# Moving the second half of a nested closing unit behind the next slot's first unit, its GpSimd adds behind the copy of x, and four weight differences one slot earlier

## The chip, the cores and the metric

The kernel runs on one core of one Trainium2 chip. The metric is the device time of one execution in microseconds (us); the median of 3 runs of the kernel before is 207.39 us (207.31 to 207.75). Times with a place, such as "94.92", are microseconds from the start of the profiled span of the kernel before.

## The reference, cut to what matters

Two blocks follow each other. The first is a cross attention without projections between `x` (8 batches, 8 heads, 512 rows, 64 wide) and `state` (32 rows per head), in both directions. The second is one exact-GELU feed-forward layer on all 4352 rows, 512 to 2048 to 512 wide.

```
a  = softmax(x @ state.T / sqrt(64));   xread = a @ state      # 512 rows per batch
a2 = softmax(state @ x.T / sqrt(64));   sread = a2 @ x         # 32 rows per batch
rows = concat([xread, sread]) with the heads side by side      # (8*544) x 512
out  = gelu_exact(rows @ w_in) @ w_out                         # (8*544) x 512
```

## The kernel before, in words

**Slots and pairs.** The work is written out by hand, engine by engine, in the order of the calls; no scheduler moves it. The main loop (L1240) has one slot for each batch b = 2 to 7, and a slot has eight pairs p = 0 to 7. In a pair `M(k, k+1)` runs two of the sixteen chunks of the first layer: `mm1` (L501) does two 128x512 matmuls of the folded weights `P` with the transposed attention `AT` into one PSUM tile `hp`, and ScalarE's GELU (L513) writes a chunk of `g`. Four PSUM buffers, tag "f", are handed out in turn to `hp`, to the scores `pt`, to the small transposes `srT` and to others: the fifth request waits until the first buffer has been read.

**The second layer, one slot later.** While slot b makes its own `g`, its pairs also multiply the `g` of batch b - 1 by `w_out`. This is done with seven products of half-size quarters in place of eight (Strassen in Winograd's form). A product is called a unit, "1" to "7"; `X(b, name)` (L676) runs one as 16 matmuls of 128x256 (`x_mm`, L648) into one of four PSUM banks (`BANK`, L667). Units "1", "6" and "7" add up in bank 1, "5" and "3" in bank 2, "2" has bank 0, "4" bank 3. What goes into "5", "6", "7" and "3" are sums of quarters of `g`, made on VectorE by `g_sum` (L633, tile `gsum`, three buffers); VectorE also adds PSUM and saved parts into the output tile `oh` (L670). Pairs 0 to 3 of a slot run units "1", "6", "5", "7" of the batch before, pair 5 unit "3".

**Nested units.** Units "2" and "4" of the later batches are themselves done with seven quarter-size products of 4 matmuls each, 128x128 (`sub_mm`, L728). Unit "4" belongs to batch 3 and later. It has three parts. `sub_sums` (L720) makes the sums of `g` (tile `gsub`). `sub_a` (L742) runs four products into the four parts of the bank, and ScalarE copies the bank to `qa` (L747). `sub_b` (L749) runs the other three products onto the same bank, ScalarE copies it to `qb` (L755), and three adds (L765) join `qa` and `qb` into `c2` or `c4`: on VectorE for unit "2", on GpSimd for unit "4". `qa`, `qb`, `c2` and `c4` have one buffer each, shared by both units. The sub-products need differences of weights, `q_w`, made once by four VectorE subtractions for each unit (`w_subs`, L590).

**Order around the change.** In slot b: pair 3 has `sub_sums(b, "2")`; pair 5 `sub_a(b, "2")` and `sub_sums(b, "4")`; pair 6 `sub_b(b, "2")`; pair 7 `sub_a(b, "4")`. Pair 0 of slot b + 1 has `M`, then `sub_b(b, "4")`, then `g_sum` of "5" and "6", then unit "1". Pair 1 starts with the scores of the next batch (`scores`, L325: exponentials on ScalarE, L340, with a load of its activation table before them and another before the next GELU), pair 2 and 3 have `norm` (L347: reduce, reciprocal, product `a<-e,ics` at L356), pair 2 of an odd slot the transposes `srT` (`srts`, L421). `c4` is read by `c21` (L709) after unit "7" in pair 3. Slot 7 has its own order for pairs 0 to 4 (`read_out_slot`, L1044), where the 32 read-out rows of all batches go through the same layer: `SR` (L862) with sums `srx` (L842), `srw` (L825) and `srt` (L885 to L898).

**GpSimd's queue.** GpSimd also brings in `x`: `hold_for` (L1032) waits for a given GELU, `load_x` (L115) issues the 512 KB load `xb`, `rearr` (L221, copies at L225) and `rearr_ones` (L230, copies at L235) copy it into the two layouts `x` and `xo`. In pair 0 of a slot the order on GpSimd is: the adds of unit "4", `hold_for` and `load_x`, `rearr` of batch b + 2.

Of the kernel before, what the change touches and what calls it, by code (L numbers as in the profile page):

```python
# [9 lines left out]
FP32 = mybir.dt.float32  # L10
# [7 lines left out]
def kernel(  # L18
# [562 lines left out]
    QN = NH // 2  # L581
# [94 lines left out]
    def X(b, name):  # L676
        bank = BANK[name]
        first = name in "2154"
        if first:
            xs[b, bank] = otile([128, 2, NH], "xp", bank)  # L680
        ps = xs[b, bank]
        x_mm(ps, x_lhs(b, name), w_rhs(name), first)
        if name == "2":
            if b > 1:
                snap(b, "c2", "c2", ps)
        elif name == "4":
            snap(b, "c4", "c4", ps)
        elif name == "1":
            for h in range(2):
                xs[b, "o", h] = hpool.tile([128, 2, d_model], FP32, name="oh", tag=f"oh{h}")  # L690
            add(xs[b, "o", 0][:, :, left], ps, xs[b, "c2"])
            x_out(b, 0, left)
        elif name == "6":
            snap(b, "u", "u", ps)
        elif name == "5":
            snap(b, "s5", "c2", ps)
        elif name == "7":
            if b < B - 2:
                c22(b)
                c21(b)  # L700
                x_out(b, 1)
        elif name == "3":
            add(xs[b, "o", 0][:, :, right], ps, xs[b, "u"])
            x_out(b, 0, right)
# [44 lines left out]
    def sub_b(b, unit):  # L749
        sub_mm(b, unit, "6", 1)  # L750
        sub_mm(b, unit, "3", 3)
        sub_mm(b, unit, "7", 0, True)
        qa = xs[b, "qa"]
        qb = cpool.tile([128, 4, QN], FP32, name="qb", tag="qb")
        nc.scalar.copy(out=qb, in_=xs[b, BANK[unit]])  # L755
        name = "c" + unit
        c = xs[b, name] = c_tile(name)
        c = c.rearrange("p j (n w) -> p j n w", n=2)
        wide = [128, 2, QN]
        for out, x, y in (  # L760
            (c[:, 0], qb[:, 1:2, :].broadcast_to(wide), qb[:, 0:4:3, :]),
            (c[:, 1], c[:, 0, 0:1, :].broadcast_to(wide), qa[:, 2:4, :]),
            (c[:, 0, 0, :], qa[:, 1, :], qa[:, 0, :]),
        ):
            (nc.vector if unit == "2" else nc.gpsimd).tensor_tensor(out=out, in0=x, in1=y, op=ALU.add)  # L765
# [76 lines left out]
    def sr_x(names):  # L842
        for name in names:
            if "x" not in sr:
                t = att.tile([128, 4, 2, TH], BF16, name="srx", tag="e")
                one = att.tile([128, 2, TH], BF16, name="srx1", tag="a")
                sr["x"] = dict(zip("34167", [t[:, i] for i in range(4)] + [one]))
            (k0, n0), (k1, n1), op = {
                "3": ((0, 1), (1, 1), ALU.subtract),
                "4": ((1, 0), (0, 0), ALU.subtract),  # L850
                "6": ((0, 0), (0, 1), ALU.add),
                "1": ((0, 0), (1, 1), ALU.add),
                "7": ((1, 0), (1, 1), ALU.add),
            }[name]
            nc.vector.tensor_tensor(
                out=sr["x"][name], in0=sr_xq(k0, n0), in1=sr_xq(k1, n1), op=op
            )
# [186 lines left out]
    def read_out_slot(p):  # L1044
        c, b, k = B - 2, B - 1, 16 * (B - 1) + 2 * p
        if p == 0:
            sr_x("34")
            M(k, k + 1)
            sub_b(c, "4")
            g_sum(c, "56")  # L1050
            SR("3", 0)
            SR("4", 0)
            X(c, "1")
            sr_x("167")
            SR("5", 0)
            SR("2", 0)
            sr_w("7")
        if p == 1:
            M(k, k + 1)
            SR_gelu("52", 0)  # L1060
            X(c, "6")
            SR("1", 0)
            SR("6", 0)
        if p == 2:
            M(k, k + 1)
            SR_gelu("6", 0)
            SR("7", 0)
            SR_gelu("7", 0)
            g_sum(c, "7")
            X(c, "5")  # L1070
            SR("3", 1)
            SR("4", 1)
            g_sum(c, "3")
        if p == 3:
            M(k, k + 1)
            SR("5", 1)
            SR("2", 1)
            SR_gelu("52", 1)
            X(c, "7")
            c22(c)  # L1080
            SR("1", 1)
            c21(c)
            x_out(c, 1)
            SR("6", 1)
        if p == 4:
            M(k, k + 1)
            SR_gelu("6", 1)
            SR("7", 1)
            SR_gelu("7", 1)
            X(c, "3")  # L1090
# [149 lines left out]
    for b in range(2, B):  # L1240
        nb = b + 1
        for p in range(8):
            k = 16 * b + 2 * p
            if p == 1 and nb < B:
                scores(nb, 0)
                scores(nb, 1)
            if p in (2, 3) and nb < B and (b > 2 or p == 2):
                norm(nb, p - 2)
            if p == 3 and nb + 1 < B:
                xtr_dma(nb + 1)  # L1250
            if p == 5 and nb < B:
                atr_dma(nb)
            if nb == B and p < 5:
                read_out_slot(p)
                if p == 4:
                    r_homes()
                    r_sum("56")
                continue
            late = p == 5 and b % 2 and nb < B
            if late:  # L1260
                M(k)
            elif b != 2 or p != 3:
                M(k, k + 1)
            if b == 2 and p == 2:
                M(k + 2, k + 3)
            if b == 2 and p == 1:
                w_diff("7")
            if p < 5 and nb < B:
                if p == 0:
                    if b > 3:  # L1270
                        sub_b(b - 1, "4")
                    g_sum(b - 1, "56")
                if p == 2:
                    if b % 2:
                        srts((b - 1, b))
                    g_sum(b - 1, "7")
                if p == 3:
                    g_sum(b - 1, "3")
                if p < 4:
                    X(b - 1, "1657"[p])  # L1280
                if p == 3:
                    sub_sums(b, "2")
                    if b == 3:
                        w_subs("4", range(4))
                if b == 2 and p == 2:
                    norm(3, 1)
                    for x in [(2, f, p_mm(2, f, ftile)) for f in (2, 3)]:
                        p_copy(*x)
                if p == 1 and b > 2:
                    sr_w("5216"[b - 3])  # L1290
            if p == 0 and b + 3 < B:
                hold_for(b, 0)
                load_x(4 if b == 2 else b + 3)
            if p == 6 and b == 2:
                hold_for(b, 12)
                load_x(5)
            if p == 0 and nb + 1 < B:
                begin(nb + 1)
                rearr(nb + 1)
            if nb == B:  # L1300
                if p == 5:
                    R("2")
                    r_sum("73")
                    R("4")
                    sub_sums(b, "2")
                if p == 6:
                    R("1")
                    sub_a(b, "2")
                    R("6")
                    sub_b(b, "2")  # L1310
                    R("5")
                if p == 7:
                    X(b, "4")
                continue
            if p == 5:
                X(b - 1, "3")
                if late:
                    M(k + 1)
                reads = (b, nb) if b % 2 == 0 else ()
                rest = p_all(nb, reads)  # L1320
                if b == 2:
                    rearr_ones(4)
                elif nb + 1 < B:
                    if not reads:
                        hold_for(b, 11)
                    rearr_ones(nb + 1)
                sub_a(b, "2")
                if b > 2:
                    sub_sums(b, "4")
                for _, f, ps in rest:  # L1330
                    nc.scalar.copy(out=Ps[nb][:, 0, f * 512:(f + 1) * 512], in_=ps[0])
            if p == 6:
                sub_b(b, "2")
            if p == 7:
                if nb == B - 1:
                    srts(reads)
                if b > 2:
                    sub_a(b, "4")
                else:
                    X(b, "4")  # L1340
# [43 lines left out]
```

## Time and profile before

| | us |
|---|---|
| median of 3 runs (lowest, highest) | 207.39 (207.31, 207.75) |
| the profiled execution's own time | 207.22 |
| its span, first to last instruction | 205.4 |
| TensorE (PE) busy | 194.1 (94% of the span) |
| VectorE (DVE) busy | 163.3 (80%) |
| ScalarE (ACT) busy | 147.8 (72%) |
| GpSimd (POOL) busy | 58.2 (28%) |
| granted TensorE clock, mean | 1.000 |

The lines of the timeline read: start, length, engine, line of the code, operation, output<-inputs, shapes, count of merged instructions, and in square brackets how long the engine had been idle before and on what. A matmul's length holds the time through the array, so the next one starts before its end; what a group of matmuls costs TensorE is the distance from its start to the start of the next group. By that measure in slot 4: a pair `M` 0.86, a whole unit 1.75, the scores 0.47, a `sub_b` 0.67 (94.92 to 95.59). "PEld" is the load of weights, "SPq" the queue that issues transfers.

### The profile page before, as it was taken

The numbers are of one execution on the slowest core, as the hardware profiler recorded it, in microseconds if no ns is written. First come the engines' busy times: TensorE is split into PE (matmuls) and PEld (weight loads), VectorE is DVE, ScalarE is ACT, GpSimd is POOL, SyncE is SP. The second block draws the span as 40 slices with busy tenths as digits, with TensorE's granted clock in tenths as the row PEclk, the third lists the DMA queues.
The fourth block names the chain that finished last, engine by engine and source line by source line (L and its number), as shares of the span: only waits on it lengthen the run. The fifth ranks groups of instructions, "written<-read, shape, count | busy, mean of one in ns | idle before, by whom it ended". The sixth has DMA issues, their size and how long they took to land.

```text
span 205.4 us, 5204 instructions
## 1 busy us (share of the span) xinstructions
PE 194.1 (94%) x2155; PEld 134.0 (65%) x2155; DVE 163.3 (80%) x299; ACT 147.8 (72%) x268; POOL 58.2 (28%) x77
## 2 busy tenths in 40 slices
PE   7899999999999999988999899989999899999992
PEld 2434544466766777656767577657776688878891
DVE  2954895889988699986998889978977987984952
ACT  3775678798984998489966996689849778765120
POOL 8972503634332423041803081213000220000000
PEclk9999999999999999999999999999999999999999
DMA  6999999988467899440597015821033010030153
GB/s 199 197 168 203 209 196 188 186 145 149 52 121 192 120 119 215 133 99 3 95 160 207 2 56 102 130 77 39 15 121 86 3 51 3 35 120 3 51 154 108
DMA packets 40569, 23.19 MB, mean 113 GB/s; under 512 B 21856, under 2 KB 39136, under 8 KB 40544
## 3 DMA queue, kind: packets, MB, share of 16 engines
q0 software_dynamic: 13984, 8.10, 29.4%
q1 hardware_dynamic: 25728, 14.22, 28.1%
q10 hardware_dynamic: 832, 0.52, 0.8%
q8 instruction: 17, 0.28, 0.6%
q14 instruction: 8, 0.07, 0.1%
HBM read 17.30 MB, written 8.91 MB: 128 GB/s over the span
## 4 chain that ended last, share of the span: by engine, by line
PE 78%; ACT 5%; DMA 5%; DVE 5%; POOL 4%; issue 1%; ACTq 0%; POOLq 0%; DVEq 0%
PE xp L651 31%; PE hp L506 22%; PE xp L733 7%; DMA xb<-in_x_dram 5%; PE op L548 4%; PE sp L877 3%; PE rp L949 3%; DVE c L765 2%; POOL w_in_bf L105 2%; PE op L532 2%; PE xp L784 2%; PE pt L333 2%; ACT g L513 2%; PE p_ps L441 1%; ACT qa L747 1%; PE sr L979 1%
## 5 line engine op out<-in xcount | busy, mean ns | idle before, releaser
L513 ACT ACTIVATE g<-hp 128x512 bf16<-128x512 f32 x124 | 67.1, 613 | 16.9 <-PE hp L506 16.7
L506 PE MATMUL hp<-AT,P 128*128 128x512 bf16 x248 | 62.2, 379 | 0.0
L651 PEld LDWEIGHTS <-gsum 128*128 128x128 bf16 x416 | 40.4, 98 | 8.9 <-issue 0.4
L651 PE MATMUL xp<-ws,gsum 128*128 128x256 bf16 x320 | 38.2, 273 | 0.0
L506 PEld LDWEIGHTS <-P 128*128 128x128 bf16 x248 | 22.8, 98 | 19.3 <-ACT P L452 0.7
L670 DVE TENSOR_TENSOR oh<-xp,c 128x512 f32<-128x512 f32 (+1 forms) x22 | 14.2, 663 | 6.7 <-PE xp L651 5.1
L651 PEld LDWEIGHTS <-g 128*128 128x128 bf16 x176 | 16.9, 98 | 2.7
L225 POOL COPY x<-xb 128x1024 bf16<-128x1024 bf16 x12 | 12.6, 1080 | 18.5 <-DMA xb<-in_x_dram 18.5
L641 DVE TENSOR_TENSOR gsum<-g 128x2048 bf16<-128x2048 bf16 x14 | 17.0, 1217 | 0.6 <-ACT g L513 0.6
L235 POOL COPY xo<-xb 128x1024 bf16<-128x1024 bf16 x12 | 12.2, 1047 | 11.8 <-PE sr L979 11.6
L651 PE MATMUL xp<-w_out_bf,g 128*128 128x256 bf16 x128 | 15.3, 273 | 0.0
L733 PE MATMUL xp<-q_w,gsub 128*128 128x128 bf16 x120 | 11.6, 219 | 3.6 <-ACT qa L747 3.6
L765 POOL TENSOR_TENSOR c<-qb 128x256 f32<-128x256 f32 x4 | 3.7, 923 | 39.8 <-ACT qb L755 39.8
L733 PEld LDWEIGHTS <-gsub 128*128 128x128 bf16 x160 | 10.2, 97 | 6.6 <-issue 5.3
L356 DVE TENSOR_TENSOR a<-e,ics 128x512 bf16<-128x512 bf16 x14 | 12.6, 900 | 0.5
L548 PE MATMUL op<-w_out_bf,g 128*128 128x512 bf16 x48 | 11.8, 380 | 0.0
L651 PE MATMUL xp<-w_out_bf,gsum 128*128 128x256 bf16 x96 | 11.5, 272 | 0.0
L1019 DVE CAST P<-p_ps 128x512 bf16<-128x512 f32 x15 | 9.4, 684 | 2.1 <-PE p_ps L441 2.1
L1033 POOL COPY hold<-g 128x1 bf16<-128x1 bf16 x7 | 2.8, 404 | 28.7 <-ACT g L513 28.7
L353 DVE TENSOR_REDUCE cs<-e 128x16 f32<-128x512 bf16 x14 | 9.5, 677 | 0.7 <-ACT e L340 0.7
L441 PE MATMUL p_ps<-w_in_bf,sbd 64*32 64x512 bf16 x248 | 9.2, 380 | 0.7 <-DVE oh L670 0.7
L674 ACT COPY c<-xp 128x512 f32<-128x512 f32 x10 | 6.0, 596 | 4.8 <-PE xp L651 4.6
(156 smaller groups left out, 334.3 us busy)
## 6 DMA issues: line engine op xcount, KB each, us to landing
out_dram<-oh SPq DMA_DIRECT2D x15, 256.0 KB, 2.7
xb<-in_x_dram POOLq DMA_DIRECT2D x7, 512.0 KB, 6.9
out_dram<-oh SPq DMA_DIRECT2D x6, 512.0 KB, 3.3
w_in_bf<-in_moe_w_in_dram POOLq DMA_DIRECT2D x6, 256.0 KB, 12.2
out_dram<-osb SPq DMA_DIRECT2D x5, 256.0 KB, 2.9
w_out_bf<-in_moe_w_out_dram POOLq DMA_DIRECT2D x4, 256.0 KB, 7.8
w_out_bf<-in_moe_w_out_dram POOLq DMA_DIRECT2D x2, 512.0 KB, 13.6
x0f<-in_x_dram SPq DMA_DIRECT2D x3, 256.0 KB, 3.9
```

Of the source, the lines that this page charges most:

```text
L225: nc.gpsimd.tensor_copy(out=A.x4[:, :, :, 64 * t:64 * t + 64].rearrange("p j c d -> p c j d"), in_=src[:, t],)
L235: eng.tensor_copy(out=A.xo[:, :, :, 2 + 64 * t:66 + 64 * t].rearrange("p j c d -> p c j d"), in_=src[:, t],)
L353: nc.vector.reduce_sum(out=cs, in_=e4, axis=AX.X)
L356: nc.vector.tensor_tensor(out=A.a[:, :, hs].rearrange("p g (c n) -> p g c n", n=NS), in0=e4, in1=ics[:, :, :].to_broadcast((128, G, 2, NS) ...
L441: nc.tensor.matmul(ps[t][32 * c:32 * c + 32, :], lhsT=sbd[64 * t:64 * t + 64, b, c, 32 * t:32 * t + 32], rhs=w_in_bf[64 * t:64 * t + 64, c ...
L506: nc.tensor.matmul(hp, lhsT=Ps[b][:, t, m * 128:(m + 1) * 128], rhs=atts[b].AT[:, :, t, :], start=(t == 0), stop=(t == 1),)
L513: nc.scalar.activation(out=gs[b][:, m, :], in_=hp, func=AF.Gelu)
L548: nc.tensor.matmul(ops[b, j], lhsT=gs[b][:, m, j * 128:(j + 1) * 128], rhs=w_out_bf[:, m, :], start=(m == 0), stop=(m == MC - 1),)
L641: nc.vector.tensor_tensor(out=got[name], in0=x, in1=y, op=op)
L651: nc.tensor.matmul(ps[:, j - js[0], :], lhsT=lhs[:, m, 128 * j:128 * j + 128], rhs=rhs[:, m, :], start=(first and j == js[0] and m == 0), ...
L670: nc.vector.tensor_tensor(out=out, in0=x, in1=y, op=ALU.add)
L733: nc.tensor.matmul(xs[b, BANK[unit]][:, at, :], lhsT=lhs[:, m, :], rhs=rhs[:, m, :], start=(start and m == 0), stop=(m == MH // 2 - 1), sk ...
```

## The change

`sub_b` is cut in two: the matmuls and ScalarE's copy to `qb` stay in it, the three adds become `sub_c`. For unit "2" both are called where `sub_b` was. For unit "4":

- in slots 4 to 6, `sub_b(b - 1, "4")` moves from before `g_sum` and unit "1" to after unit "1" of pair 0; `sub_c(b - 1, "4")` goes to pair 1, after unit "6", and so stands behind `hold_for`, `load_x` and `rearr` in GpSimd's queue (slot 5 has only `rearr`, slot 6 none of the three);
- in slot 7 (`read_out_slot`) both move behind `SR("3")`, `SR("4")` and unit "1";
- `w_subs("4", range(4))`, the four weight differences, moves from pair 3 of slot 3 to pair 6 of slot 2, ahead of `sub_b(2, "2")`.

No instruction is added or taken away on any engine, and no transfer.

```diff
         sub_mm(b, unit, "7", 0, True)
-        qa = xs[b, "qa"]
-        qb = cpool.tile([128, 4, QN], FP32, name="qb", tag="qb")
+        qb = xs[b, "qb"] = cpool.tile([128, 4, QN], FP32, name="qb", tag="qb")
         nc.scalar.copy(out=qb, in_=xs[b, BANK[unit]])
+
+    def sub_c(b, unit):
+        qa, qb = xs[b, "qa"], xs[b, "qb"]
         name = "c" + unit
...
             M(k, k + 1)
-            sub_b(c, "4")
             g_sum(c, "56")
             SR("3", 0)
             SR("4", 0)
             X(c, "1")
+            sub_b(c, "4")
+            sub_c(c, "4")
             sr_x("167")
...
                 if p == 0:
-                    if b > 3:
-                        sub_b(b - 1, "4")
                     g_sum(b - 1, "56")
...
                     X(b - 1, "1657"[p])
+                if b > 3 and p == 0:
+                    sub_b(b - 1, "4")
+                if b > 3 and p == 1:
+                    sub_c(b - 1, "4")
                 if p == 3:
                     sub_sums(b, "2")
-                    if b == 3:
-                        w_subs("4", range(4))
...
                     sub_b(b, "2")
+                    sub_c(b, "2")
...
             if p == 6:
+                if b == 2:
+                    w_subs("4", range(4))
                 sub_b(b, "2")
+                sub_c(b, "2")
```

## The prediction

> **What bounds the kernel now.** First the page's busy times: TensorE works 194.1 of 205.4 us, so what counts is where it waits. Then the list of waits, TensorE's part:
>
> ```profile
> PE xp L733 <- ACT qa L747: 3.6, 4, 0.9
> ...
> PE p_ps L441 <- DVE oh L670: 0.7, 1, 0.7
> ```
>
> Behind the start-up these five are all. Then the timeline around them. Slots 3 and 4:
>
> ```profile
> 86.19 0.42 DVE L599 TENSOR_TENSOR q_w<-ws 128x512 bf16<-128x512 bf16 x1
> ...
> 87.66 0.68 DVE L670 TENSOR_TENSOR oh<-xp,u 128x512 f32<-128x512 f32 x1
> ...
> 88.40 0.41 PE L441 MATMUL p_ps<-w_in_bf,sbd 64*32 64x512 bf16 x8 [0.72 <-DVE oh L670]
> ...
> 92.96 1.03 PE L506 MATMUL hp<-AT,P 128*128 128x512 bf16 x4
> ...
> 94.29 0.59 ACT L747 COPY qa<-xp 128x512 f32<-128x512 f32 x1 [0.36 <-DVE c L765]
> ...
> 94.92 0.38 PE L733 MATMUL xp<-q_w,gsub 128*128 128x128 bf16 x4 [0.94 <-ACT qa L747]
> ```
>
> At 88.40 a matmul waits for a VectorE add that stands behind the four weight differences. At 94.92 `sub_b` waits for the `qa` copy, which waits for the adds of unit "2". It repeats at 117.23, 139.04 and 161.24.
>
> **What each wait costs.** `M` takes 0.86, so without a wait TensorE goes on at 92.96 + 0.86 = 93.82, not 94.92: 1.10 us, and the same in slots 5 and 6 (117.23 - 116.13, 139.04 - 137.94); 161.24 - 160.25 = 0.99 in slot 7. For 88.40 I compare with slot 5, built alike without the differences: from the pair's `hp` to the first L733 it takes 132.85 - 131.10 = 1.75, here 88.74 - 86.31 = 2.43. So 0.68 can go; the next limit is ScalarE's first `P` copy. All together 3 x 1.10 + 0.99 + 0.68 = 4.97.
>
> **Differences in slot 2.** They go ahead of the adds at 71.37, before which VectorE is idle for 1.85 on `qb`. In slot 3 the four take 87.74 - 86.19 = 1.55. They fit with 0.3 to spare; without that cover at most 1.1 would show (1.55 less 0.44 that unit "6" at 76.19 leaves after the add ending 75.75). Cost 0, gain **0.68**.
>
> **New order in slots 4 to 6**, on slot 4's clock: unit "1" 93.82 to 95.57 (`qa` is there at 94.88), `sub_b` (0.67) to 96.24, scores to 96.71, `M` 97.57, unit "6" 99.32, `M` 100.18, unit "5" 101.93, `M` 102.79, unit "7". VectorE's chain starts from `qb` of unit "2" as before, so the second `gsum` still ends at 96.65; the `oh` add no longer waits 0.89 for unit "1", ends at 97.25, and unit "6" can start at 97.57.
>
> Queued behind the moved `qb` copy on ScalarE are two table loads, the exponentials and the GELUs:
>
> ```profile
> 118.16 0.59 ACT L755 COPY qb<-xp 128x512 f32<-128x512 f32 x1
> 118.76 1.28 ACT L340 ACT_TABLE_LOAD   x1
> ...
> 121.19 1.28 ACT L513 ACT_TABLE_LOAD   x1
> ...
> 122.48 1.09 ACT L513 ACTIVATE g<-hp 128x512 bf16<-128x512 f32 x2
> ...
> 123.59 0.28 PE L424 MATMUL srT<-ident,srm 128*128 128x128 bf16 x2
> ```
>
> `qb` starts 0.26 after TensorE leaves `sub_b` (95.85 - 95.59); its start to the end of the two exponentials is 2.5 and 3.0, of the two GELUs 4.9 and 5.4, of `u` 5.9. New start 96.24 + 0.26 = 96.50, so 99.0, 99.5, 101.4, 101.9, 102.4. Four PSUM buffers go round: the pair at 99.32 (second half 99.75) needs the exponentials, that at 101.93 (102.36) the GELUs, unit "7" at 102.79 needs `u`. All hold, with 0.2 to 0.5 to spare. But in slot 5 `srT` asks for the buffer of the first GELU at 100.18 and gets it at 101.4 plus a wake-up of some 0.05: a new wait of 1.3 in place of the one removed. **Slot 5: 1.10 - 1.3 = -0.2.** Slots 4 and 6 have no `srT`.
>
> **VectorE and GpSimd in slot 4.** Unit "7" needs the third `gsum`, and it is only just in time today: 102.53 + 1.21 = 103.74, for a unit starting at 103.89. What makes it late is GpSimd:
>
> ```profile
> 98.14 1.59 DVE L837 TENSOR_TENSOR srw<-w_in_bf 128x1024 bf16<-128x1024 bf16 x2
> ...
> 100.03 2.03 POOL L225 COPY x<-xb 128x1024 bf16<-128x1024 bf16 x2
> ...
> 100.65 1.95 DVE L356 TENSOR_TENSOR a<-e,ics 128x512 bf16<-128x512 bf16 x1
> ...
> 102.53 1.21 DVE L641 TENSOR_TENSOR gsum<-g 128x2048 bf16<-128x2048 bf16 x1
> ```
>
> L356 takes 0.69 in slot 6, where GpSimd is quiet, and 1.95 here, ending 0.53 after the two copies end. Reduce, reciprocal and adds from PSUM keep their times beside GpSimd. So a VectorE operation with both inputs in SBUF and a GpSimd operation take turns. Today GpSimd's adds fall mostly on VectorE's wait and the `oh` add. After the change `hold_for` (its GELU ends 95.37, 0.13 to wake) comes after the second `gsum`, the load's issue takes 0.9, the copies come at 97.6 and the adds behind them, 4 us in one piece against `srw`, L356 and the third `gsum`. With no contention `gsum` ends 101.8 and the full 1.10 is won. If both copies keep the turn, as L356's row has it: first `srw` to 97.85, copies to 99.9, second `srw` 100.5, first add 101.2, second add 102.05 with L356 waiting, L356 102.65, third add 103.1, `gsum` 104.3: 0.45 later than today. If the turn changes at each instruction, as at 120.44, where an add of GpSimd got in between two L837: second `srw` between the copies, L356 at 100.45, `gsum` 103.0, unit "7" at 103.1, so 103.89 - 103.1 = 0.8 won. The first row is the same pair of instructions, the second the longer mix; I take **slot 4: 0**, ends -0.45 and +1.1.
>
> The Trainium skill, "SBUF", section "Who interferes with whom", says that whoever issues first holds the shared ports for its whole instruction. By that rule the second copy, issued at 101.01 after L356 had waited since 100.65, should have lost; the row says it won. By the rule slot 4 would win 0.8, by the row lose 0.45.
>
> In slot 5 the copies now wait for nothing before them but slot 4's own and move up into its end, where VectorE has 0.54 idle before 115.28. **Slot 6** has the adds alone: taking turns from 141.2, L356 ends 145.5, `gsum` 146.7, unit "7" is due at 102.79 + 44.12 = 146.91. Just free: **+1.10**, bounds 0.3 (a margin missed by 0.8, one GpSimd add) and 1.10.
>
> **Slot 7.** `SR("3")` now stands where `sub_b` stood and needs `srx`:
>
> ```profile
> 160.60 0.59 ACT L747 COPY qa<-xp 128x512 f32<-128x512 f32 x1 [0.36 <-DVE c L765]
> 160.86 0.49 DVE L855 TENSOR_TENSOR srx<-XSR 128x256 bf16<-128x256 bf16 x2
> ```
>
> Its first half ends 161.16, as late as `qa` (161.19). So the 0.99 is waited all the same: gain 0. And the adds of unit "4" move from 162.8 to 165.4 (`sub_b` now ends 164.53, `qb` 0.26 + 0.59 later). There `srt` (L891, L894) and two `srw` follow each other on VectorE, and the add behind them ends 169.44 for `SR("7")` at 169.81. No row shows an f32 operation with both inputs in SBUF beside GpSimd: the bounds are 0 (not held) and -0.9 (every turn lost: 1.2 late less 0.37 spare). Nearest is L356, same size, two SBUF inputs, held up. With the 0.2 that the earlier `oh` add gives back I take **-0.7**.
>
> **Sum.** 0.68 + 0 - 0.2 + 1.10 - 0.7 = 0.88 gained. The profiled execution took 207.22 (span 205.4 and 1.8 around it): 206.34. The median shown is 207.39, 0.17 above it; I put the forecast at **206.4**.
>
> **Rivals.**
> - Turns fall well for VectorE: slot 4 wins 0.8 to 1.1 and slot 7 loses nothing: 0.68 + 0.95 - 0.2 + 1.1 = 2.5, so 204.8. For it: 120.44. Against: 100.65. Chance 0.22.
> - All five waits simply go: 207.3 - 5.0 = 202.3. Against it are the ring at `srT` and `srx`; chance 0.04.
> - The change doesn't do what it says: each wait comes back on the next thing due (`gsum`, `srT`, `gsum`, `srx`), leaving slot 3's 0.68 less slot 7's 0.7: 207.3. Chance 0.16.
> - Slower, by GpSimd's adds and copies against VectorE: all 1.9 of adds in front of the third `gsum`. Slot 4: work alone ends 101.3, plus 3.95 of GpSimd is 105.25, 1.4 later than today; slot 6: 0.3 won; slot 7: -0.9. With 0.68 - 0.2 that is -1.5: 208.8. It decides once slots 4 and 6 together win less than 0.2. Chance 0.13.
> - The forecast itself, 205.9 to 206.9: chance 0.45.
>
> **How the numbers follow.** The range leaves out 202.3 and the far side of the slow case: 204.6 to 207.6. About 0.2% (0.4 us) is what a measurement of this kernel can tell from no change. Faster: 0.45 + 0.22 + 0.04 = 0.71; the same 0.16; slower 0.13.
>
> **What the changed profile would show.** No TensorE wait on `qa` and none on `oh` at L441; L733 1.75 after `hp` in slot 3; a wait of about 1.3 of `srT` on a GELU in slot 5; slot 6 from 22.31 to 21.2 long; in slot 4 a wait of unit "7" on `gsum`; in slot 7 one of `SR("3")` on `srx` and one of `SR("7")` on `srt`. I am wrong if the `qb` copy lets the table load start sooner, if GpSimd's copies lose their turns, or if the f32 operations do not take turns at all.

## The result, and the profile after

The changed kernel takes **206.01 us** in the median of 7 runs (205.63 to 206.56); the kernel before took 207.39 (206.89 to 208.05, 7 runs). The ratio is 0.993, with a 95% interval of 0.9909 to 0.9951. The profiled execution of the changed kernel took 206.01, its span 204.2. Times with a place are from now on microseconds from the start of the span of the kernel named.

The list of waits, TensorE's part, behind the start-up:

```profile
PE xp L651 <- DVE gsum L641: 1.1, 1, 1.1
PE srT L424 <- ACT g L513: 1.1, 1, 1.1
PE sp L879 <- ACT qa L747: 0.8, 1, 0.8
```

The four waits on `qa` before `sub_b` and the wait on `oh` before L441 are gone. Three others stand in their place: unit "7" on its sum in slot 4, `srT` on a GELU in slot 5, `SR("3")` in slot 7. Slot 6 has none. The list counts a wait from the modelled end of the last matmul. From start to start, as the prediction counts, the three are 0.16 to 0.17 longer: 1.28, 1.27 and 0.96.

The start-up ahead of slot 3 ends at another time in each profile (71.46 to 73.46), since the waits for the first `x` differ (in e5, the latest, one of them takes 1.4). So I compare lengths of slots, from the start of the `hp` pair that opens one to the start of the next; for slot 7 to the start of the last `oh` add, because the stores behind it vary too. From there to the end of the span it is 3.81 to 4.02 in all profiles but one, which comes under e5. All lengths of the study stand here:

| kernel | slot 3 | slot 4 | slot 5 | slot 6 | slot 7 to the last `oh` |
|---|---|---|---|---|---|
| before | 20.71 | 22.31 | 21.81 | 22.31 | 42.04 |
| after | 20.02 | 22.52 | 21.97 | 21.21 | 42.22 |
| e1_weights_only | 20.03 | 22.31 | 21.81 | 22.31 | 42.05 |
| e2_units_only | 20.71 | 22.50 | 21.97 | 21.21 | 42.22 |
| e3_srt_bank | 20.02 | 22.51 | 20.72 | 21.21 | 42.23 |
| e4_copy_first | 20.02 | 21.54 | 21.97 | 21.21 | 42.23 |
| e5_slot7_unit_first | 20.02 | 22.50 | 21.97 | 21.21 | 42.05 |
| e7_srx_first | 20.02 | 22.53 | 21.97 | 21.21 | 41.64 |
| e8_adds_later | 20.02 | 21.95 | 21.97 | 21.22 | 42.22 |
| e9_adds_first | 20.02 | 21.14 | 21.97 | 21.21 | 42.21 |
| e10_three_undone | 20.02 | 22.69 | 20.71 | 21.21 | 41.65 |
| e11_adds_late_slot7 | 20.02 | 22.68 | 20.71 | 21.21 | 41.06 |
| e12_load_last | 20.02 | 21.43 | 21.97 | 21.21 | 42.22 |
| e13_load_last_all | 20.02 | 23.70 | 22.26 | 21.21 | 41.06 |

A length that nothing touches repeats within 0.03 from one profile to the next, so a tenth of a microsecond in a slot can be read, though whole runs of one kernel differ by 1 us and more. From before to after: 0.69 won in slot 3, 0.21 lost in slot 4, 0.16 lost in slot 5, 1.10 won in slot 6, 0.18 lost in slot 7, together 1.24. The two spans differ by 1.2, the medians by 1.38.

Slot 3 in the timeline of the changed kernel:

```profile
86.40 0.59 PE L506 MATMUL hp<-AT,P 128*128 128x512 bf16 x2
...
86.92 1.16 PE L441 MATMUL p_ps<-w_in_bf,sbd 64*32 64x512 bf16 x32
...
88.15 0.61 PE L733 MATMUL xp<-w_out_bf,g 128*128 128x128 bf16 x8
```

The L441 matmuls run in one piece, and the first L733 comes 88.15 - 86.40 = 1.75 after the `hp`; before it was 2.43.

Slot 4, pair 0 and 1:

```profile
94.90 1.19 POOL L1035 COPY hold<-g 128x1 bf16<-128x1 bf16 x1 [4.73 <-ACT g L513]
...
96.03 0.88 POOL L117 DMA_DIRECT2D xb<-in_x_dram  x1
...
96.56 4.05 DVE L839 TENSOR_TENSOR srw<-w_in_bf 128x1024 bf16<-128x1024 bf16 x2
...
96.90 2.03 POOL L225 COPY x<-xb 128x1024 bf16<-128x1024 bf16 x2
...
98.89 1.17 POOL L767 TENSOR_TENSOR c<-qb 128x256 f32<-128x256 f32 x1
...
101.53 0.75 DVE L356 TENSOR_TENSOR a<-e,ics 128x512 bf16<-128x512 bf16 x1
...
102.20 1.21 DVE L641 TENSOR_TENSOR gsum<-g 128x2048 bf16<-128x2048 bf16 x1
...
103.47 0.72 PE L651 MATMUL xp<-ws,gsum 128*128 128x256 bf16 x5 [1.12 <-DVE gsum L641]
```

The hold lies beside the second `gsum` (94.82 to 96.04) and takes 1.19, so the load is issued at 96.03 only. Two `srw` take 4.05 us; elsewhere one takes 0.68 (76.27 before). Taken apart, the first runs from 96.56 to 99.48 and ends 0.55 behind the second copy of `x`, which ended at 98.93. All behind it on VectorE is late, and unit "7" starts at 103.47. Without a wait it was due 102.79 - 92.96 = 9.83 after the slot's start by the prediction, so at 102.19: it is 1.28 late, more than the 1.10 that the slot had won.

Slot 5:

```profile
118.41 0.59 ACT L754 COPY qb<-xp 128x512 f32<-128x512 f32 x1 [0.41 <-PE xp L733]
...
122.71 1.08 ACT L513 ACTIVATE g<-hp 128x512 bf16<-128x512 f32 x2
...
123.36 0.27 PE L424 MATMUL srT<-ident,srm 128*128 128x128 bf16 x2 [1.10 <-ACT g L513]
```

`srT` starts as the first of the two GELUs ends (122.71 + 0.6): it waits for that GELU's PSUM buffer. The pair before it starts at 121.23, so without a wait `srT` was due at 122.09: it is 1.27 late.

Slot 7:

```profile
159.53 0.49 DVE L857 TENSOR_TENSOR srx<-XSR 128x256 bf16<-128x256 bf16 x2
...
159.88 1.07 PE L879 MATMUL sp<-srx,w_in_bf 128*128 128x128 bf16 x16 [0.80 <-ACT qa L747]
...
164.56 0.83 DVE L893 TENSOR_TENSOR srt<-srt 128x512 f32<-128x512 f32 x1 [0.34 <-ACT srt L892]
...
165.50 1.03 DVE L896 TENSOR_TENSOR srt<-srt 128x512 f32<-128x512 f32 x1
...
166.46 1.54 DVE L839 TENSOR_TENSOR srw<-w_in_bf 128x1024 bf16<-128x1024 bf16 x2
...
167.92 1.47 DVE L900 TENSOR_TENSOR srt<-sp,srt 128x512 f32<-128x512 f32 x2
...
168.65 0.61 PE L879 MATMUL sp<-srx,srw 128*128 128x128 bf16 x8
```

And `SR("7")` with the add that it waits for in the kernel before:

```profile
168.75 1.48 DVE L898 TENSOR_TENSOR srt<-sp,srt 128x512 f32<-128x512 f32 x2
...
169.81 0.61 PE L877 MATMUL sp<-srx,srw 128*128 128x128 bf16 x8
```

`SR("3")` starts 159.88 - 158.06 = 1.82 after the slot's start; without a wait it would be 0.86. L893 and L896 lie beside GpSimd's adds (164.12 to 166.85) and take 0.83 and 1.03 in place of 0.68; the first `srw` behind them takes 0.94 in place of 0.68. The add that `SR("7")` waits for, the first of the two L900, ends at 168.60, or 10.54 after the slot's start; before it was 169.44, or 10.05.

### The profile page after: what moved, and what is told of

It reads as the page before. It is cut to its first block, busy times and chain, and to the rows that moved or that the text cites. A ratio compares the mean times of both kernels' runs of the same rounds, so it can differ in the third digit from the quotient of the medians.

```text
span 204.2 us, 5204 instructions
## 1 busy us (share of the span) xinstructions
PE 194.5 (95%) x2155; PEld 134.1 (66%) x2155; DVE 166.4 (81%) x299; ACT 147.5 (72%) x268; POOL 60.2 (29%) x77
## 4 chain that ended last, share of the span: by engine, by line
PE 76%; ACT 6%; DVE 6%; DMA 5%; POOL 4%; issue 1%; DVEq 0%; POOLq 0%; ACTq 0%
PE xp L651 28%; PE hp L506 22%; PE xp L733 7%; DMA xb<-in_x_dram 5%; PE op L548 4%; PE sp L879 3%; PE rp L951 3%; DVE srw L839 2%; POOL w_in_bf L105 2%; PE op L532 2%; PE xp L786 2%; ACT g L513 1%; ACT P L1021 1%; PE p_ps L441 1%; DVE gsum L641 1%
## 5 line engine op out<-in xcount | busy, mean ns | idle before, releaser
L1035 POOL COPY hold<-g 128x1 bf16<-128x1 bf16 x7 | 3.4, 481 | 35.3 <-ACT g L513 35.3
L733 PE MATMUL xp<-q_w,gsub 128*128 128x128 bf16 x120 | 11.6, 219 | 0.0
L733 PEld LDWEIGHTS <-gsub 128*128 128x128 bf16 x160 | 10.2, 98 | 1.5 <-issue 0.5
L356 DVE TENSOR_TENSOR a<-e,ics 128x512 bf16<-128x512 bf16 x14 | 10.6, 754 | 0.5
L726 DVE TENSOR_TENSOR gsub<-g 128x512 bf16<-128x512 bf16 x20 | 9.2, 458 | 0.0
L441 PE MATMUL p_ps<-w_in_bf,sbd 64*32 64x512 bf16 x248 | 9.1, 380 | 0.0
```

Source lines behind the costliest of these rows:

```text
L356: nc.vector.tensor_tensor(out=A.a[:, :, hs].rearrange("p g (c n) -> p g c n", n=NS), in0=e4, in1=ics[:, :, :].to_broadcast((128, G, 2, NS) ...
L441: nc.tensor.matmul(ps[t][32 * c:32 * c + 32, :], lhsT=sbd[64 * t:64 * t + 64, b, c, 32 * t:32 * t + 32], rhs=w_in_bf[64 * t:64 * t + 64, c ...
L733: nc.tensor.matmul(xs[b, BANK[unit]][:, at, :], lhsT=lhs[:, m, :], rhs=rhs[:, m, :], start=(start and m == 0), stop=(m == MH // 2 - 1), sk ...
```

## The experiments

Each edit is against the changed kernel, unless another is named. Each time stands beside runs of the kernel before on the same chip: 207.06 for the first four, 207.36 for e5, e7, e8 and e9, 206.99 for e10 to e12, 207.45 for e13. The changed kernel was not run again there, so against it I go by the slots of the profiles, one for each kernel.

**e1_weights_only** and **e2_units_only**: the two parts of the change by themselves.

```diff
 e1, against the kernel before
-                    if b == 3:
-                        w_subs("4", range(4))
...
+                if b == 2:
+                    w_subs("4", range(4))
                 sub_b(b, "2")
```

> The kernel before, with the four weight differences moved to pair 6 of slot 2 and nothing else. My theory (each part of the change acts alone, at its own place): the wait at L441 in slot 3 goes, from the pair's hp to the first L733 takes 1.75 in place of 2.43, and the time falls by 0.6 to 0.7, to about 206.7; the four waits of sub_b on qa stay as they are (1.10, 1.10, 1.10, 0.99). Rival A (what VectorE is spared in slot 3 it is charged in slot 2 or takes back later): 207.4.

Measured: 206.49, ratio 0.9973 (0.9955 to 0.999). Slot 3 is 20.03 long, all others are as before, and the four waits on `qa` are there.

> The changed kernel with the weight differences back in pair 3 of slot 3: the reordering of unit 4 alone. My theory: slot 6 is 1.1 shorter than before, slots 4 and 5 are 0.2 longer each, slot 7 about 0.15 longer, so 0.5 to 0.6 is won: 206.8. Rival B (the whole gain is that of the weights, the reordering gives nothing): 207.4, with slot 6 at 22.3.

Measured: 206.67, ratio 0.9976 (0.996 to 0.9992). Slot 3 is 20.71 again with its wait of 0.72 at L441; the other slots are those of the changed kernel within 0.02. The two parts win 0.69 and 0.57 by the slots, against 1.24 together: they add up and do not touch each other.

**e3_srt_bank**: `srT` of slot 5 does not take its turn among the four buffers "f", but lies in a bank that is free at that time.

```diff
-    def srts(bs):
-        ps = ps_f.tile([128, len(bs), HC, NS], BF16, name="srT", tag="f")
+    def srts(bs, pool=ps_f, tag="f"):
+        ps = pool.tile([128, len(bs), HC, NS], BF16, name="srT", tag=tag)
...
-                        srts((b - 1, b))
+                        srts((b - 1, b), *((ps_o, "o0") if b == 5 else ()))
```

> The changed kernel with the two transposes srT of slot 5 written to PSUM bank 0, which is idle there, and not to one of the four buffers that go round; the order of instructions is the same on every engine. My theory (srT waits for the buffer that the late GELU holds, and for nothing else): the 1.10 wait goes, slot 5 shrinks from 21.97 to 20.8 to 20.9, the time to 204.9. Rival C (ScalarE itself is behind there, by the two table loads after the qb copy): the next pair of M or unit 7 waits instead, slot 5 stays at 21.5 or more, 205.6 to 206.0.

Measured: 204.56, ratio 0.987 (0.9852 to 0.9888). Slot 5 goes from 21.97 to 20.72, and no wait takes the place of the one removed. The late GELU held only a buffer; nothing else on TensorE needed it by then.

**e4_copy_first**: in slot 4 GpSimd copies `x` ahead of the hold and the load, so before the GELU that the hold waits for.

```diff
+            if p == 0 and b == 4:
+                begin(nb + 1)
+                rearr(nb + 1)
             if p == 0 and b + 3 < B:
                 hold_for(b, 0)
...
-            if p == 0 and nb + 1 < B:
+            if p == 0 and nb + 1 < B and b != 4:
```

> The changed kernel with the two copies of x in slot 4 ahead of hold_for and load_x in GpSimd's queue, so that they need not wait for the slot's first GELU and run near 90 in place of 97. Same work on every engine. My theory (the third gsum of slot 4 is late because copies and adds of GpSimd take turns with VectorE's operations from SBUF): the 1.12 wait of unit 7 goes, slot 4 falls from 22.52 to about 21.3, the time to 204.8; some 0.2 may be lost where the copies now meet gsub near 90. Rival D (VectorE has too much work in slot 4 whatever GpSimd does): slot 4 keeps 22.3 or more, 206.0.

Measured: 204.76, ratio 0.9884 (0.9867 to 0.9901). Slot 4 is 21.54 long, 0.98 shorter than in the changed kernel. The copies now meet the `gsub` sums of the slot before:

```profile
89.56 1.00 DVE L726 TENSOR_TENSOR gsub<-g 128x512 bf16<-128x512 bf16 x1
90.21 2.42 POOL L225 COPY x<-xb 128x1024 bf16<-128x1024 bf16 x2
90.59 1.14 DVE L726 TENSOR_TENSOR gsub<-gsub,g 128x512 bf16<-128x512 bf16 x1
...
91.66 1.25 DVE L726 TENSOR_TENSOR gsub<-g 128x512 bf16<-128x512 bf16 x1
```

Two of them take 1.14 and 1.25 in place of 0.42; the first, with its 1.00, meets a copy `xo` and is as long in the changed kernel. Unit "6" waits 0.21 for an `oh` add. Most of slot 4's loss is the copies' place, not VectorE's work alone.

**e8_adds_later**: in slot 4 the three adds wait for a GELU of pair 2, the copies stay.

```diff
-                if b > 3 and p == 1:
-                    sub_c(b - 1, "4")
+                if b > 4 and p == 1:
+                    sub_c(b - 1, "4")
+                if b == 4 and p == 2:
+                    hold_for(b, 4)
+                    sub_c(b - 1, "4")
```

> The changed kernel with GpSimd's three adds of unit 4 in slot 4 held back to pair 2 (behind a hold on the GELU of that pair's first chunk, about 10 us after the slot's start), so that only the two copies of x lie before the third gsum. My theory (copies and adds both take turns from VectorE): the wait of unit 7 falls from 1.12 to 0.6 to 0.8, slot 4 from 22.52 to 21.9 to 22.2. Rival G (the adds alone do it): 21.3. Rival H (the copies alone do it): 22.5.

Measured: 205.16, ratio 0.9898 (0.9873 to 0.9923). Slot 4 is 21.95 long and unit "7" waits 0.52, where it waited 1.12. The first `srw` still takes 2.92. So in the changed kernel 0.57 of slot 4's length is due to the adds. A slot 4 without any wait is 22.31 - 1.10 = 21.21 long, as slot 6 is, so the other 21.95 - 21.21 = 0.74 is left to the hold, the load and the copies ahead of the adds.

**e9_adds_first**: in slot 4 the adds stand ahead of the hold, the load and the copies, as in the kernel before.

```diff
                 if b > 3 and p == 0:
                     sub_b(b - 1, "4")
+                if b == 4 and p == 0:
+                    sub_c(b - 1, "4")
-                if b > 3 and p == 1:
+                if b > 4 and p == 1:
                     sub_c(b - 1, "4")
```

> The changed kernel with GpSimd's adds of unit 4 in slot 4 ahead of hold_for, load_x and the copies of x, as in the kernel before: it tests the part of the change that puts the adds behind the copy. The same GpSimd work then meets VectorE in another order: adds against srw, copies against a and the third gsum. If a copy that is first keeps the turn for both copies, gsum ends later still and slot 4 is 22.5 to 22.9, so the order of the change is the better one; if gsum is first, it is free of them and slot 4 is 21.2 to 21.4. I hold the first for likelier (6 in 10).

Measured: 204.55, ratio 0.9887 (0.9853 to 0.9921). Slot 4 is 21.14 long, with no wait. I had thought it likelier that the slot stays at 22.5 or more; that was wrong. From the timeline of this kernel:

```profile
99.74 1.22 DVE L641 TENSOR_TENSOR gsum<-g 128x2048 bf16<-128x2048 bf16 x1
99.80 0.91 POOL L117 DMA_DIRECT2D xb<-in_x_dram  x1
100.71 2.12 POOL L225 COPY x<-xb 128x1024 bf16<-128x1024 bf16 x2
```

The adds share with the two `srw` (1.81 for both), and the third `gsum` starts 0.06 ahead of the issue of the load and runs unhindered. What this margin is worth, e10 shows. The profile is of one of four runs at 204.3 to 204.6; the two others took 205.8 and 206.1.

**e5_slot7_unit_first**: in slot 7 unit "1" ahead of `SR("3")` and `SR("4")`, so that unit "1" covers the wait on `srx`.

```diff
             g_sum(c, "56")
+            X(c, "1")
             SR("3", 0)
             SR("4", 0)
-            X(c, "1")
             sub_b(c, "4")
```

> The changed kernel with unit 1 of slot 7 ahead of SR 3 and SR 4, so that TensorE has 1.75 us of work while qa and srx are made. My theory: the wait of 0.96 behind the pair M goes, but VectorE is busy without a break from the adds of unit 2 up to SR 7 and is only 0.35 to 0.45 earlier (the idle 0.34 before the first srt operation), so SR 7 waits for its srt add instead: slot 7 and the rest fall from 46.18 to 45.7 to 45.8, the time by 0.4. Rival E (TensorE alone sets slot 7): 45.2, a gain of 0.96.

Measured: 205.02, ratio 0.9895 (0.9867 to 0.9923). Slot 7 to the last `oh` is 42.05, 0.17 shorter than in the changed kernel. The expectation counted to the end of the span, and by that measure the profile falls from 46.18 to 45.09: the rival's number, not mine. The other 0.9 lies behind the last `oh` add, where the last stores land: 3.05 from there to the end of the span, against 3.96 in the changed kernel. The instructions there are the same, so whether the edit brings this about or this one execution had it by chance stays open. What the rival says of the cause, that TensorE alone sets slot 7, is not what the profile shows. The wait of `SR("3")` is gone, but the next one is there:

```profile
PE sp L879 <- DVE srt L900: 0.8, 1, 0.8
```

`SR("4")`'s add (L900, 164.04) now stands behind the `oh` add of unit "1", and `SR("2")`, which goes on in the same bank, waits 0.83 for it. This part of slot 7 is bound by VectorE's order, not by TensorE's. `SR("7")`, which I had expected to wait, starts without one.

**e7_srx_first**: VectorE makes the copy `XSR` and the first two `srx` ahead of the three adds of unit "2", which give `qa` its buffer.

```diff
         if p == 0:
-            sr_x("34")
             M(k, k + 1)
...
                 sub_b(b, "2")
-                sub_c(b, "2")
+                if nb < B - 1:
+                    sub_c(b, "2")
             if p == 7:
                 if nb == B - 1:
                     srts(reads)
+                    sr_x("34")
+                    sub_c(b, "2")
```

> The changed kernel with srt's transposes' copy and srx of slot 7 ahead of VectorE's adds of unit 2 (the three adds and qa come 0.8 later). The profile names qa as what SR 3 waits for, the program's order says srx; both end within 0.05 of each other. My theory (srx): SR 3 starts within 0.1 of the pair M's end, at about 0.9 after the slot's start, before qa is copied; the rest up to 45.7 to 45.8 as in the run with unit 1 first. Rival F (qa): SR 3 starts only after the qa copy, some 2.6 after the slot's start, and the slot is 0.5 to 0.8 longer.

Measured: 205.08, ratio 0.99 (0.9875 to 0.9924). Slot 7 to the last `oh` is 41.64, 0.58 shorter. From the timeline of this kernel, TensorE and ScalarE:

```profile
159.26 1.06 PE L879 MATMUL sp<-srx,w_in_bf 128*128 128x128 bf16 x16
...
159.92 0.59 ACT L747 COPY qa<-xp 128x512 f32<-128x512 f32 x1 [0.67 <-PE sp L879]
...
168.43 0.61 PE L879 MATMUL sp<-srx,srw 128*128 128x128 bf16 x8 [0.43 <-DVE srt L900]
```

`SR("3")` starts 0.86 after the slot's start (158.40), without a wait, and 0.66 before `qa` is copied. So it was `srx` that it waited for. The list of waits above names `qa`: in the changed kernel the first `srx` ends at 159.82 and `qa` at 159.86, and the list put the wait down to the later of the two. Of the 0.96 won, 0.58 stay: `SR("7")` now waits 0.43.

**e10_three_undone**: e3, e9 and e7 in one kernel.

> The changed kernel with the three costs found so far taken away together: srT of slot 5 in the PSUM bank 0, the adds of unit 4 in slot 4 ahead of the hold, the load and the copies of x, and in slot 7 the XSR copy and the first srx ahead of the adds of unit 2. One by one against the changed kernel's profile they gave 21.97 - 20.72 = 1.25 in slot 5, 22.52 - 21.14 = 1.38 in slot 4 and 42.21 - 41.65 = 0.56 from slot 7's start to the last oh add. Theory (each is the last limit of its own slot): they add up to 3.2, slots 3 to 6 are 20.0, 21.15, 20.7 and 21.2 long, the rest 45.65; the time is 206.0 - 3.2 = 202.8, 0.978 of the kernel before. Rival (the shorter slots bring GpSimd's copies for slot 5 and VectorE's sums closer together, and a wait on gsum or oh comes back): 0.5 or more of it returns, 203.3 or later, and a new TensorE wait of that size stands in slot 5 or 6.

Measured: 204.17, ratio 0.9838 (0.9786 to 0.9889), 1.4 later than expected. Slots 5, 6 and 7 are as expected (20.71, 21.21, 41.65), and slot 4 is 22.69, not 21.15. The rival had looked for a loss of this size in slot 5 or 6; it is in slot 4:

```profile
99.12 0.91 POOL L117 DMA_DIRECT2D xb<-in_x_dram  x1
...
99.64 3.49 DVE L641 TENSOR_TENSOR gsum<-g 128x2048 bf16<-128x2048 bf16 x1
100.02 2.02 POOL L225 COPY x<-xb 128x1024 bf16<-128x1024 bf16 x2
```

The order of the instructions in slot 4 is that of e9. There the hold and the product L356 came at one time (99.13), the hold took 0.74, and `gsum` was 0.06 ahead of the issue. Here the hold takes 0.19, `gsum` starts within the issue, loses to both copies and takes 3.49 in place of 1.22; unit "7" waits 1.28. A tie of some hundredths on GpSimd decides 22.69 - 21.14 = 1.55 us. The six runs of this kernel spread over 3.0 us (202.28 to 205.26), those of e3 over 0.3. That the tie falls either way from run to run would fit: the runs of e9, which has the same order, lie in two groups some 1.5 apart, and those of e11 too (four at 203.3 to 203.8, two at 201.5 and 202.3). It isn't shown, since each kernel has one profile.

**e11_adds_late_slot7**: e10, and the three adds of slot 7 wait for a GELU of pair 2.

```diff
 in read_out_slot, against e10
             sub_b(c, "4")
-            sub_c(c, "4")
...
         if p == 2:
             M(k, k + 1)
+            hold_for(b, 4)
+            sub_c(c, "4")
```

> As e10_three_undone, and the three GpSimd adds of unit 4 in slot 7 held until the fifth GELU of batch 7, pair 2, so that they lie behind the srt adds that unit SR 7 needs. Theory (the f32 adds on GpSimd and the f32 srt adds on VectorE take turns and this alone makes SR 7 wait 0.43): L893 and L896 take 0.68 each, SR 7 waits for nothing, the rest is 0.3 to 0.45 shorter than in e10_three_undone, some 45.3, the time 202.4. Rival (VectorE's own chain behind gsum, srx and the oh add is that late by itself): L893 and L896 get shorter but SR 7 still waits 0.2 or more, or a unit behind it waits for a sum; the rest is within 0.15 of e10_three_undone.

Measured: 203.36, ratio 0.9797 (0.9756 to 0.9838), the best of the study. L893 and L896 take 0.69 each, `SR("7")` waits for nothing, and slot 7 to the last `oh` is 41.06, 0.59 shorter than in e10, a little more than expected. Slot 4 has the same loss as in e10, which the expected time did not count. The f32 adds of GpSimd and VectorE do take turns, and in slot 7 of e10 nothing but they made `SR("7")` late.

**e12_load_last**: the changed kernel with slot 4's load issued behind the two copies.

```diff
                 hold_for(b, 0)
-                load_x(4 if b == 2 else b + 3)
+                if b != 4:
+                    load_x(4 if b == 2 else b + 3)
...
                 rearr(nb + 1)
+                if b == 4:
+                    load_x(7)
```

> The changed kernel with slot 4's load of x issued behind the two copies of x in GpSimd's queue, not ahead of them. In the changed kernel the first srw starts at 96.56 within the issue of the load (96.03 to 96.91) and then stands behind both copies (96.90 to 98.93): 2.92 us. Theory (an issue of a load on GpSimd holds a bf16 operation of VectorE that starts within it, and two copies in a row keep the turn): the first srw is held by the copies alone and ends 0.55 behind them, some 2.1 long, and the second starts within the issue and is held by it for 0.2 to 0.3, some 0.9 long in place of 0.68; the adds start at 98.9 as before, and slot 4 is 22.3 to 22.6 long. Rival (the issue holds nothing, VectorE lost only to the copies): the second srw takes its 0.68 unless a GpSimd add meets it, and the first is as long as the time from its start to 0.55 behind the copies all the same.

Measured: 205.07, ratio 0.9893 (0.9857 to 0.9929). Slot 4 is 21.43 long, 1.09 shorter than in the changed kernel and with no wait. The theory's 22.3 to 22.6 missed, and so did what both say of the first `srw`, that it ends 0.55 behind both copies. VectorE and GpSimd in this kernel:

```profile
95.89 2.48 POOL L225 COPY x<-xb 128x1024 bf16<-128x1024 bf16 x2
...
96.43 2.49 DVE L839 TENSOR_TENSOR srw<-w_in_bf 128x1024 bf16<-128x1024 bf16 x2
...
98.32 0.88 POOL L117 DMA_DIRECT2D xb<-in_x_dram  x1
```

Taken apart, the first `srw` ends at 97.47, 0.54 behind the *first* copy (96.93), and the second copy waits for it (1.49 long, not 1.05). Here the pair did not keep the turn. Whether the issue holds an operation that starts within it stays open by this run, since the second `srw` started before the issue; it ended at 98.91, in the middle of it. The edit also brings the copies 1.0 forward (95.89, where it was 96.90).

**e13_load_last_all**: e11 with the load behind the copies, as in e12.

> As e11_adds_late_slot7, and slot 4's load of x issued behind the two copies of x. In e11_adds_late_slot7 the third gsum of slot 4 started at 99.76 within the issue (99.23 to 100.14), lost to both copies behind it and took 3.49 in place of 1.22; unit 7 waited 1.27 for it and slot 4 is 22.68 long. Theory, formed on e12_load_last (VectorE gets its turn between two copies, at the first one's end, unless the issue of a load stands directly ahead of the pair): the copies start at 99.3, the gsum is held by the first alone and ends about 101.4 to 101.5 (0.54 to 1.1 behind that copy's end, as other rows of held bf16 operations), unit 7, due at about 102.05, waits for nothing, slot 4 is 21.1 to 21.2 long and the rest as in e11_adds_late_slot7: slots 20.0, 21.15, 20.7, 21.2, rest 45.0, the time 1.5 shorter than e11_adds_late_slot7, some 201.9, a ratio of about 0.973. Rival (the pair of copies keeps the turn whatever stands ahead of it, and e12_load_last was a chance of timing): the gsum ends 1.08 behind the second copy, at 102.4, unit 7 waits 0.4 or more and slot 4 is 21.6 or longer. In both the issue of the load, at 101.4, meets the second norm's product or the fourth gsum, which may add up to 1.0 to that sum, due at unit 3 only.

Measured: 206.26, ratio 0.9925 (0.9898 to 0.9952), 4.4 later than expected. The wait on `gsum` is gone, as expected, but `gsum` won a tie against the first copy (100.52 against 100.58), so the run does not tell the theory from the rival. Slot 4 is 23.70 for another reason, in the waits, the DMA issues and the stretch of slot 5:

```profile
PE hp L506 <- DMA AT<-a: 2.4, 1, 2.4
```

```profile
xb<-in_x_dram POOLq DMA_DIRECT2D x1, 512.0 KB, 12.0
...
AT<-a SPq DMA_TRANSPOSE x1, 8.9
```

```profile
116.54:138.80 22.26, 22.19 (x218) 15.67 (x219) 16.38 (x27) 16.14 (x29) 7.09 (x8) 0.93 0.45 84
```

The last columns of the second view are the size and the time to landing, those of the third TensorE's clock, the DMA share and GB/s. With adds, hold and copies ahead of it the load is issued at 103.57, together with the transposes `xT` at 103.64. In e12 the two go out together as well, but at 98.32 and 98.40, and the load, which takes 9.4, lands at 107.7, 1.1 after `AT` is issued (106.61, landing after 4.4). Here `AT` is issued at 107.55, the load takes 12.0 and is under way until 115.6, and `AT` takes 8.9. That the sharing makes both slow is argued from these times, not shown by a run. Slot 5's first matmul waits 2.40 for `AT`. Asked for by single microseconds, the granted clock is 0.65 from 116 to 117, 0.50 from 117 to 119, 0.65 from 119 to 120, and 1.00 before and behind; over slot 5 this makes 0.93, and the slot is 1.55 longer than in e11. In seven of this kernel's twelve runs the mean clock was 0.992 (206.3 to 207.7 us), in five 1.00 (204.5 to 206.3), so its median holds both.

## Why the prediction was right, point by point

- **The differences in slot 2** (0.68 at no cost): right, 0.69, shown by e1 alone. TensorE's path in slot 3 is 1.75 from `hp` to L733, as read from slot 5 of the kernel before.
- **Slot 4** (0, ends -0.45 and +1.1): -0.21, within the ends; the term is mis-sized by 0.2. The wait foreseen is there, unit "7" on `gsum`. That the pair of copies keeps its turn (the row at 100.65) decided, and I had set it halfway against the other. The way there was another than in my sum: it let the first `srw` end ahead of the copies and L356 lose to the adds. In the run the first `srw`, though 0.34 ahead of the copies, lost to both (2.92), and L356 took 0.75. So that the 0 came as near as it did is in part luck. That the copies and the adds share the loss was right (e8: 0.57 for the adds, 0.74 for the rest), and e9 shows that adds ahead of the copies can win the whole 1.10.
- **Slot 5** (-0.2): -0.16. By the prediction's measure `srT` is 1.27 late where I had 1.3 (the 1.10 of the list is counted otherwise), and e3, which wins 1.25, shows that it is the ring alone.
- **Slot 6** (+1.10): right, 1.10, with no wait. It was less close than I had it: `gsum` ends 0.9 before unit "7" starts (145.75 and 146.68), where I had 0.2 to spare.
- **Slot 7, `SR("3")`** (waits on `srx` as long as on `qa`, gain 0): right; 0.96 waited in place of 0.99, and e7 shows that it is `srx`.
- **Slot 7, `SR("7")`** (-0.7): the step that failed in size. The slot lost 0.18 (42.22 - 42.04). That the f32 adds take turns was right (0.83 and 1.03 in place of 0.68, e11). But each lost turn was counted as a whole instruction of delay, 1.2 in all, or 1.0 with the 0.2 that the earlier `oh` add gives back. L893, L896 and the `srw` behind them lost 0.15, 0.35 and 0.26, and the add before `SR("7")` came 0.49 later than before (10.54 and 10.05), of which 0.37 was spare by my count. In the changed kernel `SR("7")` starts 10.59 after the slot's start, where the pair before it, begun at 9.54, would have let it start at 10.40: 0.19 late. The price of the adds is larger than that where TensorE is not held up ahead of them: 0.59, e10 against e11. That the wait of `SR("3")` hides the rest in the changed kernel is argued; no run takes the adds alone out of it.
- **The sum**: 0.88 predicted, 1.24 by the slots. Of the difference of 0.36, slot 7 has +0.52 and slot 4 -0.21, slots 3 and 5 +0.05. The forecast of 206.4 stood 0.4 above the median. The two errors have opposite signs, so a part of its nearness is luck. And the range, 204.6 to 207.6, holds two of the rivals as well; what tells them apart is the slots, not the time.
- **The rivals**: "turns fall well for VectorE" is refuted in slot 4 and half true in slot 7. "All five waits simply go" failed at the places named, the ring and `srx`, and at `gsum` in slot 4. "The change doesn't do what it says" held for slots 4, 5 and 7 but not for slot 6, and slot 7 did not lose the 0.7. The slower case needed slot 6 to win only 0.3 and slot 4 to lose 1.4.

## What to carry to other kernels

A wait that is removed shows its gain only as far as the next thing due: three of five waits came back on another engine's late result, and each could be named beforehand from the row that would be late next. A step moved behind a queue of long GpSimd instructions is priced by the VectorE operations it then meets, and where two operations arrive within a tenth of a microsecond, one profile is not enough to price it. Before an issue of a load is moved back, look at what else is under way on the DMA engines at its new time.

## What the runs showed of the hardware that was not expected

**A load's issue ahead of a pair of copies.** Where the issue stood directly ahead of the two copies, the VectorE operation waiting beside them lost to both: L356 at 100.65 before (1.95), `srw` at 96.56 after (2.92), `gsum` at 99.64 in e10 (3.49). Where it did not, VectorE got its turn behind the first copy: `srw` at 96.43 in e12, the `gsub` at 90.59 in e4. e12 against the changed kernel is the one direct exchange, and it moves the copies in time as well, so this is a pattern of five rows, and what in the issue brings it about is open. One row speaks for the issue itself holding a bf16 operation: in e4 a `srw` that started at 97.35, within the issue (96.81 to 97.69), took 0.87 and ended 0.53 behind it. Against it, the f32 add at 71.37 in the kernel before lay within an issue (70.95 to 71.83) and took its 0.42.

The Trainium skill, "SBUF — State Buffer", section "Who interferes with whom", has whoever issues first get the shared ports for the whole instruction. e12's row agrees: the `srw` at 96.43 waited for the copy that had started at 95.89, and the second copy waited for the `srw`. The changed kernel's row does not: its `srw` started at 96.56, ahead of both copies (96.90), and ended behind them at 99.48.

**A held operation ended less than its own length behind the copy.** It was 0.54 to 0.55 behind the copy that held it (`srw` in the changed kernel and in e12, L356 at 100.65), where it takes 0.68 or 0.69 alone; `gsum`, 1.21 alone, ended 1.08 behind in e10.

**A wait can cost more than its length.** In the profile of e13 the 2.40 us without a matmul were followed by about 3.4 us at a granted clock of 0.50, where waits of 1.1 to 1.3 in the other profiles left the clock at 1.00. It is one profile; that only seven of the twelve runs had a mean clock of 0.992 says that it does not come every time.
